# Chained attention and two mixture layers on one core: first-pass sums of layer 2's weight quarters moved between layer 2's token tiles, gate steps spread to every third product

## The chip, the cores and the metric

The kernel runs on one core of a Trainium2 chip. The metric is the device time of one execution in microseconds; lower is better. Three runs of the kernel before gave a median of 2774.18 us (2769.89 to 2777.88). The five engines are named as the profile names them: PE is the matrix engine (PEld its weight loads), DVE the vector engine, ACT the scalar engine, POOL the GpSimd engine, SP the engine that issues the DMAs.

## The reference

Three stages follow each other. All inputs are fp32, and the last stage is where the change is.

```python
x = attention(q, k, v, mem_k, mem_v)              # 4 x 8 heads, 768 positions, chunks of 32
x = (sigmoid(x @ w_gate) * (x @ w_val)) @ w_out   # 3072 tokens, 512 -> 1536 -> 512
logits = x @ w_gate                               # 8 experts
P = exp(logits - logits.max())
for _ in range(8):                                # balance rows and columns
    P /= P.sum(1, keepdims=True) + 1e-09
    P /= P.sum(0, keepdims=True) + 1e-09
    P *= N / E
for e in range(E):
    h = np.maximum(x @ w1[e], 0.0)                # 512 -> 1024
    out += P[:, e:e + 1] * (h @ w2[e])            # 1024 -> 512
```

## The kernel before, in words

An fp32 product is made of three matmuls on operands split into a high and a low part (`operand`, lines 109 to 111: ACT casts the high part, DVE or POOL subtracts it to get the low part). Products are gathered in fours into a seven-product scheme, so sums and differences of quarters of the weights and of the tokens are operands as well.

The expert stage goes over the 3072 tokens in three passes `s` of 1024 tokens. In a pass the order of work is a list of units (expert `e`, half `hf` of the hidden width), 16 in a pass (lines 928 to 949). A unit is `layer1` (line 772) and then layer 2. `layer1` has two halves `fp`; each makes seven products of six matmuls (`product`, line 791, matmul lines 796 to 798), adds them on DVE (`add`, line 801) into `ca`, `cb`, `cd`, `ce`, and splits the results into `gh` and `gl` (`emit_g`, lines 765 and 766). The first three products of the next unit's `layer1` are issued ahead of layer 2 of this unit (the `yield` at line 814).

In the first pass, `s == 0`, layer 2 is `layer2` (line 841): eight token tiles `t` of twelve matmuls each (`py`, lines 74 to 76), and DVE adds each tile times the gate into `acc` (line 858). It needs only the plain quarters of the weights, `w2a` and `w2b`. In passes 1 and 2 it is `layer2_turned` (line 879), with the seven-product scheme, which also needs the sums of quarters, `w2c` and `w2d`. All operands of the weights are made once, in the first pass, stored to DRAM, and loaded again in passes 1 and 2.

They are made by `w1_operands` (line 128) for layer 1 and `w2_get` (line 727) for layer 2. `w2_get` is called at the end of each `layer1` half. In the first pass it splits the raw weights into `w2a` and `w2b` (ACT and POOL), issues their two stores on SP, then makes four sums of quarters into `wv` on DVE (line 114, called from 741 to 744), casts them into `w2c` on ACT, subtracts on POOL into `w2d`, and issues two more stores (746, 747). The raw weights are loaded by `ask` (line 721), one unit half at a time and two ahead, into tiles of the pool `gg` with tags `sh` and `sl`, eight buffers each, which the first pass also uses for one pair of `gh` and `gl` of each half (line 828). `w2a` to `w2d` share one pool of eight buffers (line 617). `wv` shares two buffers of tag `st` with `wq`, the quarter sums of layer 1's weights (`quad`, line 100).

The gates `P` are balanced beside the first units by the generator `sinkhorn` (line 622): 17 steps, each a short chain of DVE operations with a small matmul (`pc`, line 646; at the end the transposes `pg`, line 659). `beat` (line 668) takes a step at every second call; `product` and each token tile of `layer2` call it once. What is left is taken before layer 2 of the third unit (`n == 2`, line 935). The first use of `P` on tokens is line 875.

The program is written under a planner that simulates the engines: it may issue an instruction earlier than its place in the program, on its engine, when its operands and buffers are ready and nothing earlier in the program can be issued. The order on each engine is then fixed, and an instruction waits in it for its semaphores.

Of the kernel before, what the change touches and what calls it, by code (L numbers as in the profile page):

```python
# [10 lines left out]
F32 = mybir.dt.float32  # L11
# [4 lines left out]
ALU = mybir.AluOpType  # L16
# [43 lines left out]
def moe_chain(ctx: ExitStack, tc: tile.TileContext, qkv, mask, mrow, mone, wa, wg, wb, out):  # L60
    nc = tc.nc
# [11 lines left out]
    def mm3(ps, wh, wl, xh, xl, first, last):  # L73
        nc.tensor.matmul(ps, wh, xh, start=first, stop=False)  # L74
        nc.tensor.matmul(ps, wh, xl, start=False, stop=False)  # L75
        nc.tensor.matmul(ps, wl, xh, start=False, stop=last)  # L76
# [23 lines left out]
    def quad(name):  # L100
        return rw.tile([128, 4, 256], F32, tag="st", name=name, bufs=SB_)
# [7 lines left out]
    def operand(h, l, eng, src):  # L109
        nc.scalar.copy(h, src)  # L110
        return eng.tensor_tensor(out=l, in0=src, in1=h.bitcast(F32), op=ALU.subtract)  # L111

    def combine(eng, dst, a, b, op):
        eng.tensor_tensor(out=dst, in0=a, in1=b, op=op)  # L114
# [38 lines left out]
    with ExitStack() as c1:  # L153
# [403 lines left out]
        for b in range(1, NCH // 2):  # L557
# [3 lines left out]
            for p in range(NPAIR):  # L561
                nm = f"{b}_{p}"
# [52 lines left out]
    with ExitStack() as c2:  # L615
# [50 lines left out]
        balance, beats = sinkhorn(), [0]  # L666

        def beat():
            beats[0] += 1
            if beats[0] % 2:  # L670
                next(balance, None)

        SW = 512
# [27 lines left out]
        def w2_tile(nm, q):  # L701
            return w2p.tile([128, 1024], F32R, tag="w2", name=f"w2{q}_{nm}")

        def w2_sets(dh, dl, th=None, tl=None):
            w = {"full": [(dh[:, f * 512:(f + 1) * 512], dl[:, f * 512:(f + 1) * 512]) for f in range(2)]}
            if th is not None:
                q = [(dh[:, i * 256:(i + 1) * 256], dl[:, i * 256:(i + 1) * 256]) for i in range(4)]
                t = [(th[:, i * 256:(i + 1) * 256], tl[:, i * 256:(i + 1) * 256]) for i in range(4)]
                w.update({1: q[0], 2: q[2], 3: q[3], 4: t[3], 5: t[0], 6: t[1], 7: t[2]})
            return w  # L710

        def raw_pair(nm, src):
            rs = []
            for f, k in enumerate(("sh", "sl")):
                rs.append(gg.tile([128, 512], F32, tag=k, name=f"{nm}_{f}", bufs=SHB))
                nc.sync.dma_start(out=rs[f], in_=src[:, f, :])
            return rs
# [3 lines left out]
        def ask():  # L721
            u = next(asked, None)
            if u is not None:
                nm = "_".join(map(str, u))
                raws[u] = [raw_pair(f"r{i + 1}_{nm}", wb[u[0], u[1], u[2], :, :, i, :]) for i in range(2)]

        def w2_get(s, e, hf, fp):
            nm = f"{s}_{e}_{hf}_{fp}"
            kept = w2k[e, hf, fp]
            dh, dl = w2_tile(nm, "a"), w2_tile(nm, "b")  # L730
            if s == 0:
                rs = raws.pop((e, hf, fp))[1]
                for f, r in enumerate(rs):
                    operand(dh[:, f * 512:(f + 1) * 512], dl[:, f * 512:(f + 1) * 512], nc.gpsimd, r)
                nc.sync.dma_start(out=kept[0], in_=dh.bitcast(F32))
                nc.sync.dma_start(out=kept[1], in_=dl.bitcast(F32))
                th, tl = w2_tile(nm, "c"), w2_tile(nm, "d")
                b11, b12, b21, b22 = (r[:, d * 256:(d + 1) * 256] for r in rs for d in range(2))
                v = quad(f"wv{nm}")
                ce = nc.vector  # L740
                combine(ce, v[:, 0], b12, b11, ALU.subtract)
                combine(ce, v[:, 1], v[:, 0], b22, ALU.subtract)
                combine(ce, v[:, 2], b22, b12, ALU.subtract)
                combine(ce, v[:, 3], b21, v[:, 1], ALU.add)
                operand(th, tl, nc.gpsimd, v.rearrange("p i d -> p (i d)"))
                nc.sync.dma_start(out=kept[2], in_=th.bitcast(F32))
                nc.sync.dma_start(out=kept[3], in_=tl.bitcast(F32))
                return w2_sets(dh, dl)
            nc.sync.dma_start(out=dh.bitcast(F32), in_=kept[0])
            nc.sync.dma_start(out=dl.bitcast(F32), in_=kept[1])  # L750
            th, tl = w2_tile(nm, "c"), w2_tile(nm, "d")
            nc.sync.dma_start(out=th.bitcast(F32), in_=kept[2])
            nc.sync.dma_start(out=tl.bitcast(F32), in_=kept[3])
            return w2_sets(dh, dl, th, tl)
# [17 lines left out]
        def layer1(s, e, hf, xop, gs, w2):  # L772
# [6 lines left out]
            for fp in range(2):  # L779
# [47 lines left out]
                if not s:  # L827
                    g["21"] = emit_g(nm + "_1", tb, "s")
                w2.append(w2_get(s, e, hf, fp))
                if not s:  # L830
                    continue
# [9 lines left out]
        def layer2(s, e, hf, gs, w2, acc):  # L841
            plain = s == 0 and e == 0
            start = e == 0 and hf == 0

            def halves(t):
                return t.rearrange("p (h d) -> p h d", h=2)

            def accumulate(t, dst, src, first):
                pe = P[:, s * NTT + t, e:e + 1]
                if first and start:  # L850
                    if plain:
                        nc.scalar.copy(dst, src)
                    else:
                        nc.vector.tensor_scalar(out=dst, in0=src, scalar1=pe, scalar2=None, op0=ALU.mult)
                elif plain:
                    nc.vector.tensor_tensor(out=dst, in0=src, in1=dst, op=ALU.add)
                else:
                    nc.vector.scalar_tensor_tensor(out=dst, in0=src, scalar=pe, in1=dst, op0=ALU.mult, op1=ALU.add)  # L858

            def done(t):  # L860
                if e == E - 1 and hf == 1:
                    r0 = s * SB + t * 128
                    nc.sync.dma_start(out=out[r0:r0 + 128, :], in_=acc[t])

            for t in range(NTT):
                beat()
                py = ps_y.tile([128, DM], F32, tag="y", name=f"py{s}_{e}_{hf}_{t}")
                tt = slice((t % 4) * 128, (t % 4) * 128 + 128)
                for fp in range(2):
                    for f in range(2):  # L870
                        gh, gl = gs[fp][f"{t // 4 + 1}{f + 1}"]
                        wh, wl = w2[fp]["full"][f]
                        mm3(py, gh[:, tt], gl[:, tt], wh, wl, fp + f == 0, fp + f == 2)
                if s == 0 and e == 1 and hf == 0:
                    nc.vector.tensor_scalar(out=acc[t], in0=acc[t], scalar1=P[:, t, 0:1], scalar2=None, op0=ALU.mult)
                accumulate(t, acc[t], py, True)
                done(t)

        def layer2_turned(s, e, hf, gs, w2, acc):
# [138 lines left out]
```

## Time and profile before

| | |
|---|---|
| median of three runs | 2774.18 us (2769.89 to 2777.88) |
| profiled execution, its own time | 2767.39 us |
| its span from the first to the last instruction | 2765.6 us |
| PE busy | 2654.8 us, 96% of the span |
| DVE busy | 2118.3 us, 77% |
| ACT busy, POOL busy | 1141.4 us, 1009.4 us |
| mean granted TensorE clock | 0.988 of 2.4 GHz |

The expert stage begins at about 815 us of the span; its first pass ends at about 1460 us, and passes 1 and 2 fill the rest. Both edits act in the first pass alone. A busy share is an average over the span: what a change in the first pass is worth is read from the waits and the stretches of that pass.

### The profile page before, as it was taken

To read this page: it belongs to the slowest core of one execution; us is meant where nothing else is said; L and a number is where in the kernel's file an instruction comes from. 1 tells how busy PE (TensorE), PEld (TensorE's weight loads), DVE (VectorE), ACT (ScalarE), POOL (GpSimd) and SP (SyncE) were. 2 spreads that over 40 slices of the span, in tenths; PEclk is the share of its full clock that TensorE was granted. 3 is DMA by queue.
4 is the path that set the end of the run, shared out by engine and by line. 5 is a ranking of instruction groups with operands and counts; after the bars stand their busy time and mean duration, and the time that the engine had idled before them with its cause. 6 is when DMAs were issued, how large, how long until landed. Compare 5 with 4: busy or idle time off the path is not lost.

```text
span 2765.6 us, 38100 instructions
## 1 busy us (share of the span) xinstructions
PE 2654.8 (96%) x12917; PEld 2241.3 (81%) x12917; DVE 2118.3 (77%) x3234; ACT 1141.4 (41%) x2516; POOL 1009.4 (36%) x763
## 2 busy tenths in 40 slices
PE   7899999999988999999999999999999999999999
PEld 6798888998976778787787888888887788888887
DVE  8896678556578776767767788878888788888887
ACT  6555766655344333433434322233233423232332
POOL 4334765011034454544544233232333233232332
PEclk9899999999989999999999999999999999999999
DMA  5453667665656665766666655666556755666555
GB/s 200 157 176 127 225 224 249 211 217 171 204 189 255 230 232 211 260 223 236 243 218 239 215 191 194 226 228 219 194 197 228 263 199 192 228 228 221 193 188 190
DMA packets 260526, 586.97 MB, mean 212 GB/s; under 512 B 28873, under 2 KB 45961, under 8 KB 260332
## 3 DMA queue, kind: packets, MB, share of 16 engines
q1 hardware_dynamic: 260332, 584.54, 59.6%
q8 instruction: 102, 1.67, 0.2%
q14 instruction: 92, 0.75, 0.1%
HBM read 408.17 MB, written 176.26 MB: 211 GB/s over the span
## 4 chain that ended last, share of the span: by engine, by line
PE 58%; DVE 5%; DMA 4%; issue 1%; ACT 1%; SPq 0%; ACTq 0%; DVEq 0%
PE p L796 9%; PE p L797 9%; PE p L798 9%; PE pz L893 4%; PE pz L894 4%; PE pz L895 4%; PE py L76 4%; PE py L74 4%; PE py L75 4%; PE pzr L895 3%; PE pzr L893 3%; PE pzr L894 3%; DMA w2b<-w2k 2%; DVE wv L114 2%; DVE gl L766 2%
## 5 line engine op out<-in xcount | busy, mean ns | idle before, releaser
L796 PE MATMUL p<-xh,w 128*128 128x512 f32 x1344 | 523.9, 392 | 8.2 <-DVE cd L801 2.7
L797 PE MATMUL p<-xl,w 128*128 128x512 f32 x1344 | 525.8, 391 | 0.9 <-DVE xl L111 0.6
L798 PE MATMUL p<-xh,w 128*128 128x512 f32 x1344 | 521.7, 391 | 1.3 <-DMA w<-w1k 1.3
L796 PEld LDWEIGHTS p<-xh,w 128*128 128x128 f32 x1344 | 253.6, 189 | 64.5 <-ACT ce L818 4.1
L797 PEld LDWEIGHTS p<-xl,w 128*128 128x128 f32 x1344 | 253.8, 189 | 55.2 <-DVE xl L111 1.5
L798 PEld LDWEIGHTS p<-xh,w 128*128 128x128 f32 x1344 | 253.6, 189 | 55.2 <-DMA w<-w1k 1.8
L111 POOL TENSOR_TENSOR gl<-ce,gh 128x512 fp32r<-128x512 f32 x64 | 95.7, 1495 | 461.2 <-ACT gh L110 425.2
L901 DVE TENSOR_TENSOR acc<-pz,acc 128x512 f32<-128x512 f32 x248 | 170.2, 687 | 79.2 <-PE pz L895 77.2
L111 POOL TENSOR_TENSOR sl<-cb,sh 128x512 fp32r<-128x512 f32 x64 | 86.9, 1357 | 386.6 <-ACT sh L110 294.4
L76 PE MATMUL py<-w2a,gl 128*128 128x512 f32 x512 | 199.1, 394 | 17.6 <-DVE gl L766 17.6
L74 PE MATMUL py<-w2a,gh 128*128 128x512 f32 x512 | 201.3, 393 | 0.0
L75 PE MATMUL py<-w2b,gh 128*128 128x512 f32 x512 | 200.4, 391 | 0.0
L901 DVE TENSOR_TENSOR acc<-pzr,acc 128x512 f32<-128x512 f32 x248 | 164.9, 686 | 36.2 <-PE pzr L895 34.8
L818 ACT COPY ce<-p 128x512 f32<-128x512 f32 x96 | 56.4, 588 | 252.1 <-PE p L798 243.9
L111 POOL TENSOR_TENSOR w2d<-wv,w2c 128x1024 fp32r<-128x1024 f32 x32 | 77.0, 2406 | 197.6 <-ACT w2c L110 193.1
L250 POOL TENSOR_TENSOR sm<-sm,rs 96x512 f32<-96x512 f32 x64 | 75.4, 1196 | 196.8 <-DVE rs L248 135.7
L858 DVE SCALAR_TENSOR_TENSOR acc<-py,logit,acc 128x512 f32<-128x512 f32 x112 | 81.4, 747 | 84.9 <-PE py L76 84.9
L76 PEld LDWEIGHTS py<-w2a,gl 128*128 128x128 f32 x512 | 96.8, 189 | 43.0 <-DVE gl L766 23.1
L812 ACT COPY cb<-p 128x512 f32<-128x512 f32 x96 | 56.2, 586 | 176.7 <-PE p L798 176.6
L111 POOL TENSOR_TENSOR w<-wq,w 128x512 fp32r<-128x512 f32 x64 | 92.1, 1440 | 66.4 <-ACT w L110 60.7
L801 DVE TENSOR_TENSOR cd<-p,ce 128x512 f32<-128x512 f32 x96 | 66.0, 688 | 62.2 <-ACT ce L818 59.1
L75 PEld LDWEIGHTS py<-w2b,gh 128*128 128x128 f32 x512 | 97.0, 189 | 20.3
(291 smaller groups left out, 7212.1 us busy)
## 6 DMA issues: line engine op xcount, KB each, us to landing
w<-w1k SPq DMA_DIRECT2D x448, 256.0 KB
w1k<-w SPq DMA_DIRECT2D x224, 256.0 KB
r<-in_wb SPq DMA_DIRECT2D x128, 256.0 KB
w2a<-w2k SPq DMA_DIRECT2D x64, 512.0 KB
w2b<-w2k SPq DMA_DIRECT2D x64, 512.0 KB
w2c<-w2k SPq DMA_DIRECT2D x64, 512.0 KB
w2d<-w2k SPq DMA_DIRECT2D x64, 512.0 KB
w_g<-wak SPq DMA_DIRECT2D x84, 256.0 KB
```

The lines of the kernel that those rows point to most:

```text
L74: nc.tensor.matmul(ps, wh, xh, start=first, stop=False)
L75: nc.tensor.matmul(ps, wh, xl, start=False, stop=False)
L76: nc.tensor.matmul(ps, wl, xh, start=False, stop=last)
L111: return eng.tensor_tensor(out=l, in0=src, in1=h.bitcast(F32), op=ALU.subtract)
L796: nc.tensor.matmul(ps, wh[:, ks], xh, start=kk == 0 and not more, stop=False, skip_group_check=True)
L797: nc.tensor.matmul(ps, wh[:, ks], xl, start=False, stop=False, skip_group_check=True)
L798: nc.tensor.matmul(ps, wl[:, ks], xh, start=False, stop=kk == 1, skip_group_check=True)
L858: nc.vector.scalar_tensor_tensor(out=dst, in0=src, scalar=pe, in1=dst, op0=ALU.mult, op1=ALU.add)
L893: nc.tensor.matmul(ps, wh[:, ds], gh, start=fp == 0 and not more, stop=False, skip_group_check=True)
L894: nc.tensor.matmul(ps, wh[:, ds], gl, start=False, stop=False, skip_group_check=True)
L895: nc.tensor.matmul(ps, wl[:, ds], gh, start=False, stop=fp == 1, skip_group_check=True)
L901: nc.vector.tensor_tensor(out=a[q], in0=ps, in1=a[q], op=ALU.add)
```

## The change

Two edits. First, `w2_get` no longer makes the sums of quarters in the first pass; it puts the name, the raw tiles and the targets of the stores into a list `late`. A new function `w2_sums` takes the oldest entry and does what was left out, with the same instructions. `layer2` calls it after the token tiles 1 and 5, so that the sums of both halves of a unit come between the token tiles of that unit. Second, `beat` takes a step of the gate chain at calls 1, 4, 7 and so on, where it took one at calls 1, 3, 5.

```diff
         def beat():
             beats[0] += 1
-            if beats[0] % 2:
+            if beats[0] % 3 == 1:
                 next(balance, None)
...
+        late = []
+
+        def w2_sums():
+            nm, rs, kept = late.pop(0)
+            th, tl = w2_tile(nm, "c"), w2_tile(nm, "d")
+            b11, b12, b21, b22 = (r[:, d * 256:(d + 1) * 256] for r in rs for d in range(2))
+            v = quad(f"wv{nm}")
+            ce = nc.vector
+            combine(ce, v[:, 0], b12, b11, ALU.subtract)
+            combine(ce, v[:, 1], v[:, 0], b22, ALU.subtract)
+            combine(ce, v[:, 2], b22, b12, ALU.subtract)
+            combine(ce, v[:, 3], b21, v[:, 1], ALU.add)
+            operand(th, tl, nc.gpsimd, v.rearrange("p i d -> p (i d)"))
+            nc.sync.dma_start(out=kept[2], in_=th.bitcast(F32))
+            nc.sync.dma_start(out=kept[3], in_=tl.bitcast(F32))
+
         def w2_get(s, e, hf, fp):
...
                 nc.sync.dma_start(out=kept[0], in_=dh.bitcast(F32))
                 nc.sync.dma_start(out=kept[1], in_=dl.bitcast(F32))
-                th, tl = w2_tile(nm, "c"), w2_tile(nm, "d")
...
-                nc.sync.dma_start(out=kept[2], in_=th.bitcast(F32))
-                nc.sync.dma_start(out=kept[3], in_=tl.bitcast(F32))
+                late.append((nm, rs, kept))
                 return w2_sets(dh, dl)
...
                 accumulate(t, acc[t], py, True)
+                if t % 4 == 1:
+                    w2_sums()
                 done(t)
```

## Rows read from the trace of the kernel before

**Rows 1.** Busy time of PE, PEld, DVE, ACT, POOL; clock; DMA: first pass, then later.

```profile
940.00:1420.00 480.00, 463.75 (x2031) 379.98 (x2030) 349.68 (x454) 189.89 (x316) 237.99 (x161) 1.00 0.66 239
1460.00:1940.00 480.00, 476.49 (x2091) 391.29 (x2090) 380.06 (x563) 156.41 (x284) 151.73 (x112) 1.00 0.60 213
```

**Rows 2.** All waits of PE, 940 to 1460 us: total, times, longest.

```profile
PE py L76 <- DVE gl L766: 17.6, 13, 1.6
```

**Rows 3.** The chain of waits in one unit, 1090 to 1130 us: start, length, what.

```profile
...
1107.85 2.50 DVE wv L114 x2
1110.36 1.15 DVE gl L766
1111.50 1.43 DVE wv L114
...
1114.56 0.42 DVE wv L114
1115.05 0.58 ACT w2c L110
...
1116.66 2.46 DVE gl L766
1119.17 0.50 PE py L76
```

**Rows 4.** Groups of DVE, 940 to 1420 us: busy, mean ns, idle before.

```profile
L858 DVE SCALAR_TENSOR_TENSOR acc<-py,logit,acc 128x512 f32<-128x512 f32 x88 | 63.9, 747 | 66.8 <-PE py L76 66.8
L766 DVE SCALAR_TENSOR_TENSOR gl<-ca,gh 128x512 fp32r<-128x512 f32 x23 | 39.6, 1724 | 21.1 <-ACT gh L765 21.1
...
L801 DVE TENSOR_TENSOR ca<-p,ca 128x512 f32<-128x512 f32 x23 | 15.7, 683 | 3.6 <-PE p L798 3.5
```

**Rows 5.** Tile wv, 930 to 1450 us: ns min/median/max; then idle before its instructions.

```profile
L111 POOL TENSOR_TENSOR w2d<-wv,w2c x25: 2377/2404/2417, 935.2 to 1444.5; 128x1024 fp32r<-128x1024 f32 x25
...
L114 DVE TENSOR_TENSOR wv<-r,r x25: 418/1508/1512, 939.3 to 1448.4; 128x256 f32<-128x256 f32 x25
...
  PE py L75: 90.2, 13
```

**Rows 6.** All waits of PE that exceed 2.6 us in total, 810 to 940 us.

```profile
PE pc L646 <- DVE cs L643: 7.1, 3, 3.1
PE pg L659 <- DVE logit L651: 4.7, 1, 4.7
PE p L796 <- DVE cd L801: 2.7, 2, 2.4
```

**Rows 7.** Busy time and granted clock, ten microseconds each, columns as in rows 1.

```profile
820.00:830.00 10.00, 6.70 (x23) 4.80 (x22) 9.97 (x14) 5.15 (x9) 9.97 (x8) 0.84 1.02 384
...
870.00:880.00 10.00, 8.00 (x29) 6.64 (x30) 7.05 (x22) 1.55 (x3) 1.29 (x1) 0.83 0.50 179
...
900.00:910.00 10.00, 7.45 (x27) 6.12 (x28) 3.93 (x10) 1.86 (x4) 3.77 (x3) 0.83 0.19 72
```

**Rows 8.** DVE in order of time, first round of the gate chain.

```profile
817.48 1.50 DVE L114 TENSOR_TENSOR wv<-r 128x256 f32<-128x256 f32 x1
...
820.40 1.50 DVE L114 TENSOR_TENSOR wv<-r,r 128x256 f32<-128x256 f32 x1
821.82 1.51 DVE L114 TENSOR_TENSOR wv<-wv,r 128x256 f32<-128x256 f32 x1
...
823.47 0.73 DVE L114 TENSOR_TENSOR wv<-r,wv 128x256 f32<-128x256 f32 x1
...
825.57 0.51 DVE L643 TENSOR_REDUCE cs<-logit 128x8 f32<-128x192 f32 x1
```

**Rows 9.** Waits of DVE for loads of raw weights, 940 to 1420 us.

```profile
DVE wq L114 <- DMA r<-in_wb: 24.5, 11, 3.0
```

**Rows 10.** Lines 875 and 858, whole span: ns min/median/max, first and last start.

```profile
L875 DVE TENSOR_SCALAR acc<-acc,logit x8: 472/484/1040, 922.5 to 936.9; 128x512 f32<-128x512 f32 x8
L858 DVE SCALAR_TENSOR_TENSOR acc<-py,logit,acc x112: 740/750/752, 962.3 to 1530.9; 128x512 f32<-128x512 f32 x112
```

More of the change, by code (lines that the diff above doesn't have):

```diff
@@ L736, in w2_get @@
                 nc.sync.dma_start(out=kept[1], in_=dl.bitcast(F32))
-                th, tl = w2_tile(nm, "c"), w2_tile(nm, "d")
[L738 to L745, printed above, removed]
-                nc.sync.dma_start(out=kept[2], in_=th.bitcast(F32))
-                nc.sync.dma_start(out=kept[3], in_=tl.bitcast(F32))
+                late.append((nm, rs, kept))
                 return w2_sets(dh, dl)
```

## The prediction

> **What bounds the kernel now.** I read the page's busy shares first: the matrix engine is busy for 96% of the span, so only time in which it stands still or runs slowly can be won. Then the table of stretches: in 480 us of the first pass it is busy for 463.75 us, in 480 us of the second for 476.49 [rows 1]. The first pass loses 16.25 us in that stretch, the second 3.51, at a clock of 1.00 in both. Next, who waited for whom. From 940 to 1460 us the matrix engine has one kind of wait: 13 times a layer 2 matmul stood for `gl`, a low part that DVE makes, 17.6 us in all, about 1.35 us in each unit [rows 2]. The chain of waits inside one such unit says why: four `wv` sums, mixed with two other DVE operations, run from 1107.85 to 1114.98 us, then `w2c` is cast on ACT, and the `gl` that layer 2 needs begins only at 1116.66; the matmul starts at 1119.17 [rows 3]. So the instructions that the first edit moves stand on the path today.
>
> The start of the pass, 810 to 940 us, is a place of its own. There the gate chain costs 7.1 us in three waits for column sums and 4.7 us in one wait before the transposes, and two waits for `cd` cost 2.7 us [rows 6]. The longer of them also cost clock: the slices that hold them were granted 0.84, 0.83 and 0.83, so the matrix engine was at the lower of its levels, 1.2 GHz, for part of them [rows 7].
>
> **The change part by part.** The sum is made against the profiled execution, 2767.39 us, which is 6.8 us under the median of the runs, 2774.18; I add these 6.8 us at the end.
>
> *Counts.* Nothing is added or removed. There are 32 unit halves in the pass; each keeps four sums, a cast, a subtraction and two stores. What changes is their place in the program, and what SP has queued: the two stores of `w2c` and `w2d` now follow the stores of both halves' `w2a` and `w2b`. In the program each `w2c` also comes after the next unit's first three products.
>
> *The steady stall.* In the chain, the four sums take DVE's time from 1107.85 to 1110.36, 1111.50 to 1112.93 and 1114.56 to 1114.98 [rows 3], 2.50 + 1.43 + 0.42 = 4.35 us, ahead of the `ca` that feeds the late `gl`; `w2c` adds 0.58 us on ACT in front of it. The stall is 1.35 us. If one 1.43 us sum fewer stood there, the stall would be gone, and what is late next is nothing on PE's list [rows 2]. So the gain lies between 0 and 17.6 us. It is 0 if the sums end up in the same place again. That is possible, because place in the program is not all that decides: the cast of `w2c` waited 13 times, 90.2 us, for the layer 2 matmul that frees its tile [rows 5], so sums were ready well before their buffer and the planner had run them ahead. It is all of it if they go where DVE stands idle between tiles, 66.8 us over 88 tiles before the adds of line 858 [rows 4]. I take 8 us, just under half, since the trace shows both the lower priority's room and the running ahead.
>
> *The sums at their new place.* A tile of layer 2 is twelve matmuls at 480 us / 2091 = 0.23 us [rows 1], 2.75 us; its add takes 0.75 [rows 4]. One set of sums is 4 x 0.42 = 1.7 us alone (the shortest of the second sum is 418 ns) and 4 x 1.5 = 6.0 us at its median of 1508 [rows 5]. DVE has 2.0 us free in a tile, so the adds of two or three tiles could be late by up to 4 us; four banks for `py` cover three tiles, 8.2 us. I cost it at nothing; uncovered, it is at most 4.0 - 2.75 = 1.3 us for each set, as much as today's stall.
>
> *The price of a sum beside POOL.* The same sum takes 418 ns at its shortest and 1508 at its median, while `ca`, which has one operand in PSUM, stays at 683 [rows 4, 5]. The Trainium skill, page SBUF — State Buffer, section Who interferes with whom, says that a DVE instruction with two operands in SBUF and a GpSimd instruction that reads SBUF exclude each other, and that whoever comes second waits for the whole of the first. The rows agree, and the rule speaks against the move: a sum is no cheaper at its new place if POOL works there. By the rows an extra sum ahead of `ca` would cost 1.43 us [rows 3]; by the rule it could cost the whole of a `w2d`, 2.40 us [rows 5], and the second rival below would stand at 2774 + 12 x 2.40 - 5 = 2798 us.
>
> *Gate steps.* Step k comes at beat 2k - 1 before and 3k - 2 after. The first column sum (`pc`, in step 4) goes from beat 7 to 10, the last (step 14) from 27 to 40, the transposes (steps 16 and 17) from 31 and 33 to 46 and 49. Beat 58 is the last before the drain at the third unit (14 products, 3, 8 tiles, 11, 3, 8, 11), so all 17 steps still fall before it. More matmuls lie between two steps, so a late DVE operation is covered more often. What can go: the 7.1 and 4.7 us of waits [rows 6], and half of the time at 1.2 GHz, (0.16 + 0.17 + 0.17) x 10 = 5.0 us [rows 7]; together 16.8. What can be lost is as much again, since a step that now meets a busier DVE stands PE still in the same way. The first round also had four `wv` sums, 1.50 + 1.50 + 1.51 + 0.73 = 5.24 us, between its operations, and the column sum came at 825.57 [rows 8]; behind layer 2's tile 1 they are less urgent than the gate. I take a gain of 5 us, about one of the three long stands with its clock. The two waits for `cd`, 2.7 us [rows 6], are behind the same sums; I take 2. The gates are first used at 922.5 us, and by the first gated add at 962.3 [rows 10]; the last slice with a gate wait ends at 910 [rows 7], so 16 beats of at most 2.75 us, 44 us, still end before 962.
>
> *Raw tiles held longer.* The sums now read the raw weights after layer 2 has begun, so these hold their buffers for longer, and `ask` gets its buffers later. A load that waits for its buffer holds what is queued behind it on SP, the stores of layer 1's weights among it, and those free the tiles for the next half's weights. DVE already waited 24.5 us in 11 waits for raw loads [rows 9] and none of it reached PE [rows 2]. Bounds: nothing, or 11 x 1.35 us = 15 us, if each of these waits grew until it cost PE what the present stall does. I take 2 us, nearer to the row that shows it hidden.
>
> Sum: -8 - 5 - 2 + 2 = -13 us. 2767.4 - 13 = 2754.4, and with 6.8 the median is 2761 us. Its own range goes from -34 us (17.6 + 16.8, to 2740) to -6 (2768).
>
> **The rivals.** *The planner undoes the move.* `w2c` waits for buffers that layer 2's last tiles free, the sums wait for the two buffers of `wv` and `wq`, and both come free at the same moment as before. Then four sums again stand before `ca`, and only the start of the pass changes, by 5 us either way: 2774 - 4 = 2770 us. For it: the 90.2 us of the cast's waits [rows 5]. Against it: layer 1's weights now come before the sums in the program and should get the `wv` and `wq` buffers first.
>
> *Both halves' sums meet in front of `ca`.* Before, a half's sums were parted by the other half's layer 1; now a unit's two sets follow each other. If they wait for the same buffers, five or six sums rather than four run after layer 2's last tile, and each that stands before `ca` adds 1.43 us [rows 3] to a stall that is already open: 12 units x 1.43 = 17 us, less 5 at the start, 2774 + 12 = 2786 us. It decides from the first extra sum. From the second on, a stand of 1.35 + 2.9 us is longer than the 3.1 us that went with a fallen clock at the start [rows 6, 7], and each would cost about 1.7 us more, 12 x 3.1 = 37 us above that. For it: `wv` has few buffers and no slack in this place. Against it: layer 2 gives DVE idle time right after [rows 4].
>
> **How the numbers follow.** The forecast gets 0.55, the planner undoing the move 0.25, the meeting sums 0.20. A run of this kernel tells about 0.3%, 8.3 us, from no change: 2766 to 2782.5. Of the forecast's 0.55, 0.06 lies above 2766. Of the rival at 2770, nearly all is within the band, 0.01 below it and 0.01 above. So faster 0.50, same 0.30, slower 0.20. The range is 2740 to 2787: below it is the case that every stall goes and the clock holds as well, above it half of the meeting sums' case, with its clock; together 0.15.
>
> **What would show it.** Right: from 940 to 1460 us the wait for `gl` falls from 17.6 us to about 10; no `wv` on the chain of waits in front of `ca`; waits for column sums and transposes fall from 11.8 us to under 7, and the slices between 820 and 910 us are granted more than 0.84. Wrong: 1.3 us of stall in each unit with `wv` before it (the first rival); stalls of 2.7 us or more in each (the second); waits of layer 1's matmuls for `w`, which would be the raw loads; or `pc` waits of the same size at other places, which would make the gate's spacing worthless. Passes 1 and 2 should not move.

## Result, and the profile after

The changed kernel takes 2737.76 us (median of 6 runs, 2736.75 to 2746.97) against 2773.12 us before in the same comparison (6 runs, 2769.33 to 2777.88): a ratio of 0.988, with an interval of 0.9863 to 0.9898. It is faster, as forecast, but by 35 us where 13 were forecast, and 2 us below the range. The two profiled executions differ by a little less: 2767.39 and 2737.62 us, spans of 2765.6 and 2735.5 us.

First the busy time of the engines after (columns as in [rows 1]): the same stretch of the first pass, and that of the later passes shifted by 30 us.

```profile
940.00:1420.00 480.00, 480.00 (x2120) 397.44 (x2119) 309.51 (x476) 188.62 (x327) 245.52 (x166) 1.00 0.69 249
1430.00:1910.00 480.00, 476.31 (x2090) 391.01 (x2089) 385.47 (x567) 157.38 (x285) 153.09 (x115) 1.00 0.61 219
```

PE now has no gap in this stretch of the first pass: 480.00 of 480 us, where it had 463.75. The list of all waits of PE from 940 to 1460 us, which held the 17.6 us of [rows 2], is empty after.

Next the unit that answers to the chain in [rows 3]. DVE after, in order of time (start, length, what, idle time before):

```profile
1091.56 0.63 DVE L114 TENSOR_TENSOR wv<-r 128x256 f32<-128x256 f32 x1
1092.11 0.41 DVE L114 TENSOR_TENSOR wv<-r,r 128x256 f32<-128x256 f32 x1
1092.45 0.68 DVE L772 SCALAR_TENSOR_TENSOR gl<-cd,gh 128x512 fp32r<-128x512 f32 x1
1093.05 0.41 DVE L114 TENSOR_TENSOR wv<-wv,r 128x256 f32<-128x256 f32 x1
1093.39 0.68 DVE L772 SCALAR_TENSOR_TENSOR gl<-ce,gh 128x512 fp32r<-128x512 f32 x1
1093.99 0.41 DVE L114 TENSOR_TENSOR wv<-r,wv 128x256 f32<-128x256 f32 x1
1095.38 0.69 DVE L807 TENSOR_TENSOR ca<-p,ca 128x512 f32<-128x512 f32 x1 [0.98 <-PE p L804]
```

and before, in the unit of [rows 3]:

```profile
1107.24 0.69 DVE L801 TENSOR_TENSOR cb<-p,cb 128x512 f32<-128x512 f32 x1 [0.46 <-PE p L798]
1107.85 1.07 DVE L114 TENSOR_TENSOR wv<-r 128x256 f32<-128x256 f32 x1
1108.84 1.51 DVE L114 TENSOR_TENSOR wv<-r,r 128x256 f32<-128x256 f32 x1
1110.28 1.23 DVE L766 SCALAR_TENSOR_TENSOR gl<-ce,gh 128x512 fp32r<-128x512 f32 x1
1111.43 1.51 DVE L114 TENSOR_TENSOR wv<-wv,r 128x256 f32<-128x256 f32 x1
1112.86 1.77 DVE L766 SCALAR_TENSOR_TENSOR gl<-cb,gh 128x512 fp32r<-128x512 f32 x1
1114.56 0.41 DVE L114 TENSOR_TENSOR wv<-r,wv 128x256 f32<-128x256 f32 x1
1114.89 0.68 DVE L801 TENSOR_TENSOR ca<-p,ca 128x512 f32<-128x512 f32 x1
1116.66 2.45 DVE L766 SCALAR_TENSOR_TENSOR gl<-ca,gh 128x512 fp32r<-128x512 f32 x1 [1.09 <-ACT gh L765]
```

Four sums stand in front of `ca` after too, in another order (`cb` comes behind `ca`). But they take 0.63 + 3 x 0.41 = 1.86 us, where these rows have 4.50, and `ca` then waits 0.98 us for PE: DVE is early. What POOL does beside them, after:

```profile
1088.81 2.41 POOL L111 TENSOR_TENSOR w2d<-wv,w2c 128x1024 fp32r<-128x1024 f32 x1 [10.66 <-ACT w2c L110]
1091.16 0.74 POOL L111 TENSOR_TENSOR w<-r,w 128x256 fp32r<-128x256 f32 x1
1095.56 2.42 POOL L111 TENSOR_TENSOR w2d<-wv,w2c 128x1024 fp32r<-128x1024 f32 x1 [3.65 <-ACT w2c L110]
```

and before:

```profile
1104.98 2.40 POOL L111 TENSOR_TENSOR w2d<-wv,w2c 128x1024 fp32r<-128x1024 f32 x1 [10.94 <-ACT w2c L110]
1107.34 2.73 POOL L111 TENSOR_TENSOR w2b<-r,w2a 128x512 fp32r<-128x512 f32 x2
1110.04 2.62 POOL L111 TENSOR_TENSOR w<-r,w 128x256 fp32r<-128x256 f32 x2
1112.62 1.47 POOL L111 TENSOR_TENSOR w<-wq,w 128x512 fp32r<-128x512 f32 x1
```

Before, POOL works without a break from 1104.98 to 1114.09 us, all through the first three sums; after, it stands idle from 1091.90 to 1095.56 us, 3.65 us, just where they are. In the trace of the kernel before, from 930 to 1450 us, the 120 sums (`wv` and `wq`) that meet no POOL instruction take 0.41 to 0.43 us, and each of the 66 that take over 0.8 us ends 0.28 us after a POOL subtraction ends. So a sum that runs into one waits for its end.

Last the start of the pass. All waits of PE after, 810 to 940 us, that answer to [rows 6]:

```profile
PE pc L646 <- DVE cs L643: 6.3, 2, 4.5
PE p L802 <- ACT w L110: 1.9, 1, 1.9
PE p L802 <- DVE ca L807: 1.5, 2, 1.1
PE p L802 <- DVE cb L807: 1.5, 1, 1.5
```

The wait before the transposes (4.7 us) and those for `cd` (2.7) are gone; the column sums keep 6.3 of 7.1. The ten-microsecond slices after (columns as in [rows 7]):

```profile
820.00:830.00 10.00, 8.87 (x33) 6.86 (x32) 9.79 (x14) 6.22 (x13) 9.76 (x8) 0.84 1.04 393
830.00:840.00 10.00, 5.52 (x17) 4.17 (x16) 8.91 (x18) 2.44 (x4) 3.75 (x3) 0.68 0.84 331
870.00:880.00 10.00, 10.00 (x47) 8.28 (x46) 7.03 (x18) 4.33 (x7) 4.50 (x4) 1.00 0.52 209
900.00:910.00 10.00, 6.76 (x30) 4.97 (x29) 7.30 (x19) 1.43 (x3) 3.65 (x3) 1.00 0.78 270
```

Two of the three slow slices of [rows 7] now have the full 2.4 GHz; the first still has 0.84, and the one at 830 us went from 0.84 to 0.68.

**Where the 30 us of the span lie.** I cut the matmul rows of PE in both traces at the first layer 1 product of the stage and at the last layer 2 matmul of units. "Start" goes to the end of the third unit, (1, 0); then come 12 units to the end of (7, 0), the last unit, and passes 1 and 2. In us:

```
          begins   start   12 units (each)   last unit   passes 1, 2
before     815.0   162.9    509.0 (42.42)       43.6        1231.0
after      817.2   148.3    490.5 (40.88)       41.3        1233.6
gain        -2.2    14.6     18.5  (1.54)        2.3          -2.6
```

Together 30.6 us up to the last matmul. The units' gain is more than the wait that went: 1.54 us each, for a wait of 1.35 [rows 2]. In the unit of [rows 3] the matmul ahead of the wait starts at 1117.47 us and the waiting one at 1119.17, 1.70 us later, where the usual distance is 0.227; that is 1.47 us lost. The profile lists this wait as 1.31 us, because it counts from the end of a matmul drawn 0.39 us long. In the start, the row of that stretch says how its gain divides. Before and after (columns as in [rows 1]):

```profile
815.00:977.90 162.90, 144.60 (x592) 115.56 (x593) 126.79 (x215) 66.12 (x113) 79.87 (x54) 0.94 0.66 240
```

```profile
817.20:965.50 148.30, 138.23 (x586) 111.62 (x587) 116.30 (x209) 62.59 (x110) 78.03 (x54) 0.96 0.70 257
```

PE stands still for 18.3 us before and 10.1 after, and its busy time falls by 6.4 us for nearly the same matmuls, at a granted clock of 0.94 and 0.96.

### The profile page after: what moved, and what is told of

Its sections match the earlier page's. It is cut to its first block, busy times and chain, and to the rows that moved or that the text cites. A ratio compares the mean times of both kernels' runs of the same rounds, so it can differ in the third digit from the quotient of the medians.

```text
span 2735.5 us, 38090 instructions
## 1 busy us (share of the span) xinstructions
PE 2649.3 (97%) x12917; PEld 2243.0 (82%) x12917; DVE 2063.2 (75%) x3234; ACT 1131.0 (41%) x2516; POOL 1007.5 (37%) x763
## 4 chain that ended last, share of the span: by engine, by line
PE 79%; DVE 10%; DMA 6%; issue 2%; ACT 2%; SPq 1%; POOL 0%; DVEq 0%; POOLq 0%; ACTq 0%
PE p L802 10%; PE p L803 10%; PE p L804 10%; PE py L74 4%; PE py L75 4%; PE py L76 4%; PE pz L901 4%; PE pz L902 4%; PE pz L903 4%; PE pzr L903 3%; PE pzr L901 3%; PE pzr L902 3%; DMA w2b<-w2k 2%; PE px L74 2%; PE px L75 2%
## 5 line engine op out<-in xcount | busy, mean ns | idle before, releaser
L74 PEld LDWEIGHTS py<-w2a,gh 128*128 128x128 f32 x512 | 96.2, 188 | 21.3 <-DVE acc L864 1.2
```

## The experiments

Each was timed against the kernel before on one chip. Theory "order": the planner falls into one of a few repeating orders during the first units, and only in some of them PE stalls. Theory "place": the sums go to where the change puts them, and that place is better. The cuts of all runs stand in a table behind the last one.

**One edit alone.** The sums behind tiles 1 and 5, gate steps as before (the edit is made to the changed kernel):

```diff
-            if beats[0] % 3 == 1:
+            if beats[0] % 2:
```

> Only the first edit: sums after token tiles 1 and 5, gate steps at every second beat as before. Theory A (the sums' lower place in the program removes the stall of 1.35 us per unit, the gate edit only helps the start): the wait of layer 2 for gl is gone, about -21 us in the steady units, -5 at the start, near 2747. Theory B (what POOL does beside the sums decides, and that is set by the order that the planner falls into at the start, so by both edits together): four sums still stand in front of ca, beside three POOL subtractions for layer 1's weights, the stall stays at about 1 us or more per unit, and the time is 2760 to 2770.

Measured: 2749.59 us (before: 2775.94), ratio 0.9907 (0.9891 to 0.9924). No wait of PE from 965 to 1455 us, so theory A's number came, and the stall that theory B kept did not.

The gate steps alone, the sums where they were:

```diff
-            if beats[0] % 2:
+            if beats[0] % 3 == 1:
```

> Only the second edit: gate steps at every third beat, sums where they were. Theory A: steady stall as before (17 us of waits for gl), start 5 to 15 us faster, 2758 to 2768. Theory B: the order in the steady units changes too, though no sum moved in the program; the sums run beside POOL's w2d and w2b as before, so waits for gl remain, but of another size; 2750 to 2768.

Measured: 2753.83 us, ratio 0.9924 (0.9909 to 0.9938). No wait for `gl` in the later units here either, though no sum was moved and all gate steps have ended by then; both theories had waits for `gl` left, and the time is in B's range alone. Each edit alone ends the stall: 26 and 22 us, which don't add up to 48 because some 19 of them are the same.

In the kernel with the sums alone, DVE's order in front of `ca` is that of before: `cb`, two sums, `gl`, a sum, `gl`, a sum. DVE there, in order of time:

```profile
1098.29 0.69 DVE L807 TENSOR_TENSOR cb<-p,cb 128x512 f32<-128x512 f32 x1 [0.46 <-PE p L804]
1098.90 0.51 DVE L114 TENSOR_TENSOR wv<-r 128x256 f32<-128x256 f32 x1
1099.33 1.52 DVE L114 TENSOR_TENSOR wv<-r,r 128x256 f32<-128x256 f32 x1
1100.77 0.68 DVE L772 SCALAR_TENSOR_TENSOR gl<-ce,gh 128x512 fp32r<-128x512 f32 x1
1101.37 0.41 DVE L114 TENSOR_TENSOR wv<-wv,r 128x256 f32<-128x256 f32 x1
1101.71 1.77 DVE L772 SCALAR_TENSOR_TENSOR gl<-cb,gh 128x512 fp32r<-128x512 f32 x1
1103.40 0.41 DVE L114 TENSOR_TENSOR wv<-r,wv 128x256 f32<-128x256 f32 x1
1103.74 0.68 DVE L807 TENSOR_TENSOR ca<-p,ca 128x512 f32<-128x512 f32 x1
1105.46 2.48 DVE L772 SCALAR_TENSOR_TENSOR gl<-ca,gh 128x512 fp32r<-128x512 f32 x1 [1.05 <-ACT gh L771]
```

From the start of `cb` to the end of the late `gl` this takes 9.65 us. Before it took from 1107.24 to 1119.11, 11.87 us, and PE stood for some 1.3 of them; so in this order a stall begins at about 10.5 us, an estimate from this one unit. PE's own order does not explain the difference: counted from the start of `cb`, PE comes to the matmul that needs the late `gl` after 10.5 us before (with the wait taken off) and after 9.8 us with the sums alone, which is sooner. There it starts at 1108.06 us, 0.12 us after `gl` is done. The 2.2 us of difference are sums of 2.85 us rather than 4.50 and a first `gl` of 0.68 rather than 1.23. POOL beside them, in the same kernel:

```profile
1098.38 2.18 POOL L111 TENSOR_TENSOR w<-r,w 128x256 fp32r<-128x256 f32 x2
1101.52 1.41 POOL L111 TENSOR_TENSOR w<-wq,w 128x512 fp32r<-128x512 f32 x1 [0.96 <-ACT w L110]
```

POOL has no `w2b` here and stands idle for 0.96 us; `w2b` comes later, at 1107.34 us, beside the sums `wq`, for which PE never waits. The Trainium skill, page SBUF — State Buffer, section Who interferes with whom, says that a DVE instruction with two SBUF inputs contends with a GpSimd instruction that reads SBUF; these rows agree. The price that the prediction took from the rule, a whole `w2d` of 2.40 us for a sum, comes too, though not in this order. It is in the kernel with the sums in layer 1 (below), where a `wq` sum meets a second `w2d` and ends 0.29 us after it:

```profile
1101.00 2.61 DVE L114 TENSOR_TENSOR wq<-r 128x256 f32<-128x256 f32 x1
1098.55 4.77 POOL L111 TENSOR_TENSOR w2d<-wv,w2c 128x1024 fp32r<-128x1024 f32 x2 [10.43 <-ACT w2c L110]
```

A `w2b` beside the sums does not make a stall by itself. The kernel with the gate edit alone has one beside two of its sums, and no stall:

```profile
1104.96 1.46 DVE L114 TENSOR_TENSOR wv<-r 128x256 f32<-128x256 f32 x1
1106.34 1.51 DVE L114 TENSOR_TENSOR wv<-r,r 128x256 f32<-128x256 f32 x1
1104.84 2.73 POOL L111 TENSOR_TENSOR w2b<-r,w2a 128x512 fp32r<-128x512 f32 x2
```

There `cd` stands ahead of the sums and `cb` behind them, and PE comes to the late `gl` in another order; the 10.5 us hold for the order of before.

**Another place, or none.** The sums at the end of layer 1, with the new gate steps:

```diff
                 w2.append(w2_get(s, e, hf, fp))
                 if not s:
+                    if fp:
+                        w2_sums()
+                        w2_sums()
                     continue
...
-                if t % 4 == 1:
-                    w2_sums()
```

> Gate steps at every third beat; both sets of sums called at the end of layer1's second half, ahead of layer 2 and not between its tiles. Theory 'the place between the token tiles matters': the stall returns, 2755 to 2770. Theory 'the order of the four parts matters' (plain quarters of both halves first, then both sets of sums): no stall, 2735 to 2745.

Measured: 2772.64 us, ratio 0.9994 (0.9983 to 1.0005). The stall is as dear as before, 42.36 us a unit, but sits elsewhere: layer 1's matmuls wait 7.8 us for `cd` and 2.2 for `ce`, layer 2's only 0.5 for `gl`. Neither expected range holds the time; that the stall returns is what the theory of the place said.

The sums left out of the kernel before; `w2c` and `w2d` are made from `w2a`'s values:

```diff
-                v = quad(f"wv{nm}")
...
-                operand(th, tl, nc.gpsimd, v.rearrange("p i d -> p (i d)"))
+                operand(th, tl, nc.gpsimd, dh.bitcast(F32))
```

> The kernel before with the four sums of each half left out: w2c and w2d are made from w2a's values, with the same casts, subtractions and stores. If the sums in front of ca are what makes the stall, the 17.6 us of waits for gl are gone (0 to 3 us left) and the time is 2740 to 2755. If the POOL work or the order on PE makes it, over 8 us of these waits are left, and the time is over 2760.

Measured: 2743.02 us, ratio 0.9879 (0.9857 to 0.9901), no wait in the later units, 40.78 us each. The changed kernel, which does all the sums, has 40.88: in the later units their cost is hidden almost to the last tenth.

**Order against spacing.** No sum moved, a gate step at every call:

```diff
-            if beats[0] % 2:
+            if True:
```

> The kernel before with a gate step at every product, denser than before (every second) and the opposite of the change (every third). No sum is moved. Theory 'order': the planner falls into one of a few repeating orders during the first units, and the spacing of the steps only tips which; in the program as planned, this kernel's order on DVE in the later units is that of the kernel with the gate edit alone (three sums of the next unit ahead of ca, POOL's subtractions of w2b elsewhere). So no wait for gl from 965 to 1455 us, about 40.8 us a unit as there, some 19 us less than before; at the start the chain of steps has less cover, 0 to 12 us more waits. 2757 to 2769 us. Rival 'spacing': what helps in the steady units is that the steps are further apart; then a denser chain keeps the stall of 17 us and loses at the start: 2776 to 2788 us.

Measured: 2766.61 us, ratio 0.9967 (0.9952 to 0.9983). No wait for `gl`, 40.81 us a unit; the start grew to 177.5 us. All waits of PE in this kernel of more than 2.8 us in total, 812 to 965 us:

```profile
PE pc L646 <- DVE cs L643: 21.9, 6, 5.8
PE p L796 <- ACT ce L818: 5.1, 2, 2.7
```

No sum moved, every third call as in the change, one call later:

```diff
-            if beats[0] % 2:
+            if beats[0] % 3 == 2:
```

> The kernel before with a gate step at calls 2, 5, 8, ... : every third as in the change, one call later. No sum is moved. In the program as planned its order on DVE in the later units is that of the kernel before. Theory 'order': the stall is back in every unit, 42.4 us a unit, 13 waits for gl of about 1.3 us from 965 to 1455 us, and only the start gains, 0 to 6 us: 2770 to 2776 us. Rival 'spacing': every third product frees the steady units wherever it begins: no waits for gl, 40.8 us a unit, 2750 to 2757 us.

Measured: 2769.55 us, ratio 0.998 (0.9964 to 0.9996), half a microsecond under the range of theory "order" and 12 above that of its rival; 42.24 us a unit. All waits of PE in this kernel, 965 to 1455 us:

```profile
PE py L76 <- DVE gl L766: 13.2, 10, 1.5
```

The pair decides it. Denser steps end the stall and steps as far apart as in the change keep it, as each planned order said. What the gate edit does for the later units is to tip the planner's order, not to free time.

**POOL beside the sums.** In the kernel before, ACT writes a copy in place of POOL's subtraction for `w2b`:

```diff
-                    operand(dh[:, f * 512:(f + 1) * 512], dl[:, f * 512:(f + 1) * 512], nc.gpsimd, r)
+                    nc.scalar.copy(out=dh[:, f * 512:(f + 1) * 512], in_=r)
+                    nc.scalar.copy(out=dl[:, f * 512:(f + 1) * 512], in_=r)
```

> The kernel before with POOL's subtraction for w2b left out: ACT writes a second copy of the weights in its place, so the low part is not the low part. In the program as planned all four sums of the next unit still stand ahead of ca, as before (cb, wv three times, gl, wv, ca). Theory 'POOL beside the sums': the stall of 1.35 us exists because those sums run at 1.4 us each beside POOL's w2b; without it they take about 0.42 us each, 3 us less ahead of ca, and the stall is gone: no gl waits, 40.8 us a unit, 2752 to 2760 us. Rival 'four sums, or the cast on ACT ahead of gh': the stall comes from their number and from w2c's cast on ACT, which now has two more copies a half; the stall stays or grows: 42.4 us or more a unit, 2774 to 2790 us.

Measured: 2738.53 us, ratio 0.9871 (0.9843 to 0.9899): faster than expected, since the start fell too. No wait from 965 to 1455 us. The sums ahead of `ca` in one unit:

```profile
1090.18 0.43 DVE L114 TENSOR_TENSOR wv<-r 128x256 f32<-128x256 f32 x1
1090.52 0.42 DVE L114 TENSOR_TENSOR wv<-r,r 128x256 f32<-128x256 f32 x1
1090.86 1.52 DVE L114 TENSOR_TENSOR wv<-wv,r 128x256 f32<-128x256 f32 x1
1092.91 1.51 DVE L114 TENSOR_TENSOR wv<-r,wv 128x256 f32<-128x256 f32 x1
```

The first two are short, as expected. The other two now meet POOL's subtractions for layer 1's weights, so the four take 3.88 us rather than 4.50, a gain of 0.6 and not of 3. The way from `cb` to the end of the late `gl` is 9.00 us for a second reason: the `gl` of `ce` (1.23 us before) no longer stands in it. The outcome was forecast, the working was not.

The same subtraction on DVE, nothing left out:

```diff
-                    operand(dh[:, f * 512:(f + 1) * 512], dl[:, f * 512:(f + 1) * 512], nc.gpsimd, r)
+                    operand(dh[:, f * 512:(f + 1) * 512], dl[:, f * 512:(f + 1) * 512], nc.vector, r)
```

> The kernel before with w2b's subtraction done by DVE rather than POOL, nothing left out. Theory 'POOL beside the sums': the sums ahead of ca run at 0.42 us, the gl wait of the steady units goes, 40.8 us a unit, though DVE gets two more instructions of 0.7 us a half; 2752 to 2762 us, with 0 to 6 us lost at the start to the fuller DVE. Rival 'DVE's load sets it': 1.4 us more DVE work a half keeps the stall or lengthens it, 42.4 to 43.8 us a unit: 2774 to 2795 us.

Measured: 2746.52 us, ratio 0.9905 (0.9876 to 0.9934), faster than either expectation; 40.59 us a unit, the lowest of all kernels, with DVE doing more. Two waits for `gl` are left from 965 to 1455 us, 0.7 us together. The second sum takes 410/414/421 ns there (min/median/max), against a median of 1508 in [rows 5]. Neither kernel keeps DVE's order of before to the last instruction, so the two show only that the stall goes in the kernels without POOL's `w2b`; the kernel with the sums alone shows what `w2b` beside the sums costs at one and the same DVE order.

**The place between the tiles.** The changed kernel with the sums behind tiles 3 and 7:

```diff
-                if t % 4 == 1:
+                if t % 4 == 3:
```

> The changed kernel with the sums behind tiles 3 and 7 rather than 1 and 5. Theory 'order': the place between the tiles is not where the sums run (they run where buffers and operands let them), so the time is that of the changed kernel, 2735 to 2742 us, with 40.9 us a unit and no wait for gl. Rival 'place': behind the last tile the sums compete with ca and gl of the next half as before; then the stall is back in whole or part, 41.6 to 42.4 us a unit, 2747 to 2757 us.

Measured: 2740.75 us, ratio 0.9876 (0.9848 to 0.9904); 40.88 us a unit, start 147.8. These are the change's own numbers: between the tiles the place does not matter. Ahead of layer 2 it does, as the kernel with the sums in layer 1 shows.

**The start.** The changed kernel with a gate step at every fourth call:

```diff
-            if beats[0] % 3 == 1:
+            if beats[0] % 4 == 1:
```

> The changed kernel with a gate step at every fourth call rather than every third. The later units are planned in the same order as there (40.9 us a unit), so only the start can differ, 148.3 us there. Theory 'relief of the start by both': the column sums wait for a DVE chain that has other work between its operations; further apart costs nothing and may take 0 to 6 us of the 6.3 us of waits for column sums that are left: 2732 to 2740 us. Rival 'spacing only moves the waits to other places': the start goes up or down by up to 5 us as chance has it, 2735 to 2744 us. Two steps are then left for the drain ahead of the third unit's layer 2; if they stand there with nothing beside them, 5 to 10 us more: 2742 to 2748 us.

Measured: 2742.96 us, ratio 0.9889 (0.9858 to 0.9921). The start is 156.0 us, 7.7 more than with every third: waits for column sums 7.6 us, a wait before the transposes of 3.2 us again, and a clock of 0.93. The theory's range ends below it. As the third case of the expectation says, two steps are left for the drain. They are the transposes, and the 3.2 us stand before them, so this run does not part the spacing from the drain.

The changed kernel with a gate step at every call:

```diff
-            if beats[0] % 3 == 1:
+            if True:
```

> The changed kernel with a gate step at every call, the densest chain. Its later units are planned in the changed kernel's order. Theory 'order': steady 40.9 us a unit and no wait for gl, however dense the chain; the start pays for the density as it did without the move (177.5 us against 162.9), 10 to 30 us over the changed kernel's 148.3: 2748 to 2768 us. Rival 'once the sums are out of the way the chain's spacing costs nothing': start 148 to 152 us, 2737 to 2742 us.

Measured: 2760.29 us, ratio 0.9952 (0.9935 to 0.9969); 40.80 us a unit, start 170.7, with 25.0 us of waits for column sums, as theory "order" has it: the chain's density costs at the start alone.

The sums left out of the kernel before, as above, and a gate step at every third call:

```diff
-            if beats[0] % 2:
+            if beats[0] % 3 == 1:
```

> The kernel before with the sums left out altogether (w2c and w2d are made from w2a's values, with the same casts, subtractions and stores) and the gate steps at every third call. It bounds what any place of the sums can give. Theory 'the move hides the sums fully': the steady units cost 40.8 us and the start 148 us, as in the changed kernel, so 2735 to 2740 us, the changed kernel's time. Rival 'the sums still cost at their new place': the start falls to 138 to 143 us and the whole to 2725 to 2732 us.

Measured: 2747.04 us, ratio 0.9902 (0.9874 to 0.993). Both expectations missed: the units cost 40.80 us, but the start is 158.6 us, 10 more than in the changed kernel, which has the sums. So the sums' load on DVE does not set the start by itself: leaving them out gave 10.1 us with a step at every second call and 2.4 with every third.

The eight balance rounds left out, of the kernel before, of the changed kernel, and of the one with the sums alone:

```diff
-            for i in range(8):
+            for i in range(0):
```

> The kernel before with the eight balance rounds left out (the gates are the plain exponentials; the steps that remain are the maximum and the transposes). Its later units are planned in the order of the kernel before. Theory 'chain at the start': nearly all of the start's loss is the gate chain and the clock that its stands cost, so the start falls from 162.9 to 140 to 148 us, while the stall of the steady units stays (42.4 us a unit): 2750 to 2760 us. Rival 'sums at the start': the start's loss is the sums that stand ahead of other DVE work there; without the chain the start stays above 152 us, and the time above 2762 us.

> The changed kernel with the same eight rounds left out. Its later units are planned in the changed kernel's order. Theory 'chain at the start': without the chain the two kernels' starts are alike, within 3 us of each other, and what is left between them is the steady units' 18.5 us and the last unit's 2: 20 to 23 us. Rival 'sums at the start': the changed kernel stays ahead at the start by more than 5 us without the chain as well, and the two are 26 to 31 us apart.

> The kernel before with the first edit alone (the sums behind the tiles, steps at every second call) and the eight balance rounds left out. Theory 'chain first': the move of the sums gives the 4.8 us at the start that stayed between the two kernels without rounds, and the spacing gives its share only through the rounds; so the start is that of the changed kernel without rounds, 138.8 us, within 1.5 us, and the time 2754 to 2758 us. Rival 'spacing without rounds': the steps that remain (maximum and transposes) give part of the 4.8 us, and the start is 141 to 144 us.

Measured: 2776.72 us (ratio 1.0003, 0.9991 to 1.0016), 2755.91 us (0.9928, 0.9904 to 0.9953) and 2751.58 us (0.9908, 0.9892 to 0.9924). The starts are 143.6, 138.8 and 136.8 us. The whole times can't be held against the kernels with rounds (last section), the starts among themselves can: without the rounds, moving the sums gives 6.8 us and the spacing gives nothing (-2.0). The theory asked for at most 3 us between the first two and its rival for more than 5; they are 4.8 apart, between the two. The third run has a start 2.0 us below the second's where 1.5 were allowed, and a time 2.4 us under its range; as far as one trace each can tell, the difference comes from the sums.

A try at a faster version, the changed kernel with `w2b`'s subtraction on DVE (the edit of the run above, made to it):

```diff
-                    operand(dh[:, f * 512:(f + 1) * 512], dl[:, f * 512:(f + 1) * 512], nc.gpsimd, r)
+                    operand(dh[:, f * 512:(f + 1) * 512], dl[:, f * 512:(f + 1) * 512], nc.vector, r)
```

> The changed kernel with w2b's subtraction on DVE rather than POOL, nothing left out. In the kernel before, the same move brought the later units to 40.59 us each and the start to 159.1 us from 162.9. Theory 'POOL beside DVE is what is left': the start falls from 148.3 to 144 to 148 us and the units to 40.6 us: 2727 to 2736 us, below the changed kernel. Rival 'another order at the start': the planned order changes again, the chain's waits fall as chance has it, the start goes to 150 to 160 us: 2737 to 2748 us.

Measured: 2746.88 us, ratio 0.9896 (0.9879 to 0.9912), with a start of 152.7 us, as the rival had it. In the trace it is slower than the change; the intervals of the two ratios overlap. No kernel that computes everything was clearly faster than the change.

The cuts of all runs, in us. One trace stands behind each row. The stage begins between 813.6 and 819.6 us in them, though no edit is meant to move that, so 2 us in a start may be scatter.

```
                              start   each unit      what
before                        162.9     42.42        stall
after                         148.3     40.88
sums alone                    157.7     40.80
gate every third alone        161.0     40.82
sums in layer 1               157.4     42.36        stall at cd
no sums                       152.8     40.78
gate every call               177.5     40.81
gate 3n + 2                   161.5     42.24        stall
w2b copied on ACT             147.7     40.81
w2b on DVE                    159.1     40.59
tiles 3, 7                    147.8     40.88
sums moved, gate every 4th    156.0     40.97
sums moved, gate every call   170.7     40.80
no sums, gate every third     158.6     40.80
before, no rounds             143.6     42.48        stall
after, no rounds              138.8     41.31
sums alone, no rounds         136.8     41.31
after, w2b on DVE             152.7     40.95
```

## Why the prediction was wrong

**What bounds the kernel** was read rightly: the stall for `gl` in each unit and the gate chain at the start are where all of the gain lies.

**The steady stall** is the step that failed. The prediction took 8 us, "just under half", for four sums that partly return to their place. It was 18.5 us over twelve units and 2.3 in the last. Two things were off. The stall is all or nothing: the repeated unit has one order, so nearly all of the twelve lose it or nearly none does. From 965 to 1455 us there are 11 waits for `gl` before, 10 with the steps at 3n + 2 and 11 before without rounds; elsewhere there are none, or one or two of 0.5 us at most. No kernel with the rounds lies between 40.97 and 42.24 us a unit, so half was the least likely value. And its bound of 17.6 us was too low, since the units gained 1.54 us each for a wait of 1.35. That the gain came at all is in part luck: the gate edit, which was not forecast to touch these units, gives it without the move.

**The reason** was off as well. The prediction let the gain hang on how many sums still stand in front of `ca`. Four stand there after, in the unit shown, and four in the kernel with the sums alone, both without a stall. What counts is how long DVE takes to the late `gl` against what PE has to do meanwhile. In the order of before, 2.2 us of that hang on what POOL runs beside the sums: the prediction named the price (418 against 1508 ns), but used it only against the move and not to ask where `w2b` would go. In other orders, as with the gate edit alone, the same price is paid and PE does not wait.

**Gate steps** (-5) **and the waits for `cd`** (-2) were taken at 7 us; the start gave 14.6, near the bound of 16.8 for the gate. The spacing alone gave 1.9, the sums alone 5.2, so 7.5 us came only with both. Without the rounds the spacing gave nothing, so its share acts through the chain's rounds, as the prediction had it. But "more matmuls lie between two steps, so a late DVE operation is covered more often" fails as a rule: with the sums moved, every call, every second, third and fourth give starts of 170.7, 157.7, 148.3 and 156.0 us. The fourth has the transposes in its drain as well. Why the third falls best of those tried is not settled.

**Raw tiles held longer** (+2, bounds 0 to 15): the mechanism came as told, the price did not. DVE's wait for raw loads went from 24.5 us in 11 waits [rows 9] to this, after, in the same stretch of 940 to 1420 us:

```profile
DVE wq L114 <- DMA r<-in_wb: 72.5, 24, 5.3
```

None of it reached PE, whose list of waits is empty there.

**The sums at their new place** were costed at nothing, which held, for another reason: behind tiles 3 and 7 they cost the same, and the units cost 40.88 us with them and 40.78 without.

**The rivals.** "The planner undoes the move" had the right doubt, that the program's place does not decide where the sums run, and the wrong end: a planner that moves them can also land in a better order. "Both halves' sums meet in front of `ca`" did not happen: in the unit shown, four sums stand there as before, and the next set starts 29 us later (1091.56 and 1120.73 us). That one edit would do the whole steady gain through the planner was not among the rivals.

## What to carry to other kernels

Under a planner, an edit anywhere ahead of a repeated loop can change the order in which the loop settles; before a gain in the loop is put down to the edit, try an edit of the same kind that should do the opposite. In these runs the stall of a repeated unit went nearly wholly or not at all, so its chance is better split between the two ends than costed at half. When a short instruction shows two durations, look at which neighbour makes the long one, and ask of each edit where that neighbour goes.

## What the runs showed that was not expected

Without the balance rounds, matmuls were slower all through the stage at a granted clock that the rows show as 1.00. From 1500 to 1900 us the kernel before has 1740 matmuls in 396.49 us, 0.228 us each; without the rounds it has this:

```profile
1500.00:1900.00 400.00, 398.57 (x1727) 323.43 (x1726) 315.52 (x460) 121.96 (x213) 117.33 (x81) 1.00 0.58 210
```

0.231 us each, and 0.231 in the changed kernel without rounds too. It is not the chip: the change with `w2b` on DVE, timed on one chip with the third kernel without rounds, has 0.228. Passes 1 and 2 took 1253.8 and 1256.7 us rather than 1231.0 and 1233.6, which ate the 19 us that the kernel before had saved at the start. Why is not settled.
